# Diagonal tiles on ScalarE in eight instructions a stage, and seven products in the last seven pairs

## The chip, the cores and the metric

The kernel runs on one core of one Trainium2 chip. The metric is the device time of one execution in microseconds, the median over several executions. TensorE, VectorE, ScalarE, GpSimd and SyncE (SP) each work through a queue of their own, in order, and wait for one another by semaphores.

## The reference

A linear attention with decay (per head and channel) is followed by a two-layer network with a leaky ReLU:

```python
# r, k, v: (B=4, H=8, S=768, D=48); w, u: (H, D)
for t in range(S):
    cur = np.einsum('bhd,bhe->bhde', u[None] * kt, vt)
    y[:, :, t] = np.einsum('bhd,bhde->bhe', rt, state + cur)
    state = w[None, :, :, None] * state + np.einsum('bhd,bhe->bhde', kt, vt)
x = y as (B * S = 3072, H * D = 384)
h = x @ w_in                    # 384 x 2048
g = np.maximum(0.01 * h, h)
out = g @ w_out                 # 2048 x 384
```

The inputs and the output are float32; the kernel computes in bfloat16 with float32 accumulation.

## The kernel before

The 3072 rows are 24 stages (n) of 128 tokens, six for each of the four batches. A stage works on all eight heads. Two stages make a pair (m = n // 2, 12 pairs), and the network runs on pairs.

The work of a stage n is:

- `prep(n)` scales r and k by powers of the decay into `qk`; for n >= 8 (`TURNED`) a DMA transpose on SP's queue turns them into `tp`, for earlier stages TensorE and ScalarE do (`turn`).
- `prep2(n)` finds `s`, the weight of a token on its own value (the u term). For n < 8 (`DIAG`) it comes out of a product on TensorE. For n >= 8 VectorE computes it in three instructions (ku at L342, rku at L344, the sum `s_tok` at L346; two buffers of each, by n % 2), and `diag_tile(n)` writes a diagonal matrix with `s` for each head into the tile `at[n % 6]`: two GpSimd instructions (L354), each for four heads, that multiply the identity by `s`.
- `a_mm(n)` makes the scores of the eight heads on TensorE (L391), in two PSUM banks that lie side by side for n >= 8, and `a_mask(n)` moves those below the diagonal into `at` (VectorE, L401). It keeps what the tile has on the diagonal, so it comes after `diag_tile(n)`.
- `y_part(n)` multiplies `at` and the running state into y (L508), and ScalarE evicts it to `xT` (L528).
- `kv_mm(n)` and `state(n)` update the state (L425, L475 to L480); the last stage of a batch has none.

The network of a pair: `g1_pair(m, j)` for j = 0 to 7 is the first product, 48 matmuls in all (L558), each j into a bank of its own, which ScalarE evicts through the leaky ReLU (Prelu) into `gT` (L564). The second product is `second(m)`: for the pairs in `SEVEN` it is `g2_seven(m)`, else `g2(2m)` and `g2(2m + 1)`, 16 matmuls of 384 columns each (L575), evicted to `out_sb` by ScalarE (L581) and stored by SP. `g2_seven` computes the same with seven block products in place of eight, 56 matmuls of 192 columns (L639). It needs four sums of blocks of `gT` for each pair (`g_sum`, VectorE, L613), four sums of blocks of `w_out` made once (`w_sum`, L595), three evictions on ScalarE that are kept aside (`keep`, L647), three additions on VectorE that go to the output (`plus`, L670) and one plain eviction.

All instructions are written down in one order, from which each engine takes its own; waits follow from the keys that an operation reads and writes. `ORDER` writes out the start by hand, up to stage 9's scores and pair 2's first half of the second product. Then a loop runs over the pairs m = 3 to 11. In before, an iteration is: the first product of pair m; `prep2` of stages 2m + 4 and 2m + 5 (`ahead`); `g_sum` of pair m - 1 if that is in `SEVEN`; loads of stages 2m + 8 and 2m + 9 on GpSimd's queue, paced by the first product; `a_mm` and `a_mask` of `ahead`; `y_part` of stages 2m + 2 and 2m + 3; `kv_mm` and `state` of `ahead`; `prep` of stages 2m + 6 and 2m + 7; `w_sum`; and `second(m - 1)`.

The eight PSUM banks go round: every product takes the next bank (`next_bank`), and waits there for whoever still reads what that bank held. `a_mm` leaves bank 7 out where its two banks would not lie side by side (L383). Ahead of `second` the counter is turned on to the bank that y began with:

```python
        if m < NST // 2 - 1:
            while taken[0] % 8 != y_first:
                taken[0] += 1
```

Of the kernel before, what the change touches and what calls it, by code (L numbers as in the profile page):

```python
# [5 lines left out]
ALU = mybir.AluOpType  # L6
AF = mybir.ActivationFunctionType
# [4 lines left out]
B, H, S, D = 4, 8, 768, 48  # L12
# [3 lines left out]
NST = B * NC  # L16
HD = H * D
E = 64
NP = H // 2
# [4 lines left out]
FIRST, EARLY = 6, 2  # L24
# [96 lines left out]
def bass_rwkv5_eagle__then__act_leaky_relu_kernel(  # L121
# [15 lines left out]

    NQK, NTP, NVS, NAT, NT, NX, NG, NO, NRK = 6, 6, 6, 6, 6, 3, 3, 4, 14
    TURNED, DIAG = 8, 8
    SEVEN = (8,9,10,11)  # L140
    HF, NH = NFB // 2, HD // 2
    w_in_sb = SB("w_in_sb", [128, NSL, DFF])
    w_out_sb = SB("w_out_sb", [128, NFB, HD])
# [24 lines left out]
    ident = SB("ident", [128, 128])  # L168
    ku = [SB(f"ku{i}", [128, HD]) for i in range(2)]
    rku = [SB(f"rku{i}", [128, HD]) for i in range(2)]  # L170
    s_tok = [SB(f"s_tok{i}", [128, H], FP32) for i in range(2)]
# [3 lines left out]
    at = [SB(f"at{i}", [128, 2, NP, 128]) for i in range(NAT)]  # L175
# [11 lines left out]
    V, A, PE, SP, G = nc.vector, nc.scalar, nc.tensor, nc.sync, nc.gpsimd  # L187
    sch = Sched(ctx, nc)
    add = sch.add
# [79 lines left out]
    for name in LOADS.split():  # L269
# [12 lines left out]
        R=["tcol"], W=["kexp"])  # L282
    add("dve", lambda: V.tensor_scalar(qexp[:, :], tcol[:, :], 1.0, float(-MID), ALU.mult, ALU.add),
        R=["tcol"], W=["qexp"])
    add("dve", lambda: V.memset(v_sb[:, :, :].rearrange("p n (h e) -> p (n h) e", e=E)[:, :, D:E], 0.0), W=["v0"])
    add("dve", lambda: V.tensor_tensor(wu_row[:, :], w_row[:, :], u_row[:, :], ALU.mult),
        R=["w_row", "u_row"], W=["wu_row"])
    for i in range(NQK):
# [6 lines left out]
        R=["one_row", "w_row"], W=[key_w, "bc"])  # L295
# [33 lines left out]
        add("dve", lambda: V.tensor_tensor(prod[i2][:, :, :], tp[it][:, 0:NP, :], tp[it][:, NP:2 * NP, :], ALU.mult),  # L329
            R=[("tp", it, 0), ("tp", it, 1)], W=[("prod", i2)])  # L330

    def prep2(n):
        i2, iv = n % 2, n % NVS
        if n < DIAG:
            ps_s, key = kv_bank[n]
            s_of = ps_s[:, HD:HD + H]
            add("dve", lambda: V.tensor_tensor(hd(vs[iv][:, :]),
                                               v_sb[:, n, :].rearrange("p (h e) -> p h e", e=E)[:, :, 0:D],
                                               s_of.unsqueeze(2).to_broadcast([128, H, D]), ALU.mult),
                R=[("v", n), key], W=[("vs", iv)])  # L340
        else:
            add("dve", lambda: V.tensor_tensor(ku[i2][:, :], k_of(n), u_tab[:, :], ALU.mult),  # L342
                R=[("k", n % NRK), "u_tab"], W=[("ku", i2)])
            add("dve", lambda: V.tensor_tensor(rku[i2][:, :], r_of(n), ku[i2][:, :], ALU.mult),  # L344
                R=[("r", n % NRK), ("ku", i2)], W=[("rku", i2)])
            add("dve", lambda: V.tensor_reduce(s_tok[i2][:, :], hd(rku[i2][:, :]), AX.X, ALU.add),  # L346
                R=[("rku", i2)], W=[("s", i2)])
            diag_tile(n)

    def diag_tile(n):  # L350
        ia = n % NAT
        for hh in range(2):
            s_of = s_tok[n % 2][:, :].rearrange("p (m two) -> p two m", two=2)[:, hh, :]
            add("pool", lambda hh=hh, s_of=s_of: G.tensor_tensor(  # L354
                at[ia][:, hh, :, :], ident[:, :].unsqueeze(1).to_broadcast([128, NP, 128]),
                s_of.unsqueeze(2).to_broadcast([128, NP, 128]), ALU.mult),
                R=["ident", ("s", n % 2)], W=[("at", ia, hh)])

    def turn(n):
        it, iq = n % NTP, n % NQK  # L360
# [251 lines left out]
        ][i]  # L612
        add("dve", lambda: V.tensor_tensor(x[i][:, :, :], a, b, op), R=keys, W=[("gs", m % 2, i)])  # L613

    def g2_seven(m, early=(), late=()):
        ig, i2 = m % NG, m % 2
        final = m == NST // 2 - 1
        banks = [next_bank() for _ in range(4 if final else 3)]
        top, low = slice(0, HF), slice(HF, NFB)
        one, two = slice(0, NH), slice(NH, HD)  # L620

        def product(where, left, right, first, last):
            ps_o, key = banks[where]
            if isinstance(left, int):
                lhs, reads = gs[i2][left], [("gs", i2, left)]
            else:
                r, c = left
                lhs = gT[ig][:, HF * c:HF * c + HF, 128 * r:128 * r + 128]
                reads = [("gT", ig, r, j) for j in range(4 * c, 4 * c + 4)]
            if isinstance(right, int):  # L630
                rhs = tw[right]
                reads = reads + [("tw", right)]
            else:
                rhs = w_out_sb[:, right[0], right[1]]
                reads = reads + [("wout", i) for i in range(4)]

            def emit():
                for s in range(HF):
                    done = PE.matmul(ps_o[:, 0:NH], lhs[:, s, :], rhs[:, s, :], start=first and s == 0,  # L639
                                     stop=s == HF - 1, skip_group_check=not (first and last))  # L640
                return done

            add("pe", emit, R=reads, W=[key])

        def keep(where, i):
            ps_o, key = banks[where]
            add("act", lambda: A.activation(snap[i2][i][:, :], ps_o[:, 0:NH], AF.Copy), R=[key], W=[("snap", i2, i)])  # L647

        def store(r, c):
            n = 2 * m + r  # L650
            io, cols = n % NO, (one, two)[c]
            if final:
                add("sp", lambda: SP.dma_start(out[128 * n:128 * n + 128, cols], out_sb[io][:, cols]),
                    R=[("o", io, c)], W=[("out", n, c)], dma=f"o{io}{c}")
            elif (n, 1 - c) in landed:
                add("sp", lambda: SP.dma_start(out[128 * n:128 * n + 128, :], out_sb[io][:, :]),
                    R=[("o", io, 0), ("o", io, 1)], W=[("out", n, 0)], dma=f"o{io}")
            landed.append((n, c))

        def plain(where, r, c):  # L660
            ps_o, key = banks[where]
            io, cols = (2 * m + r) % NO, (one, two)[c]
            add("act", lambda: A.activation(out_sb[io][:, cols], ps_o[:, 0:NH], AF.Copy), R=[key],
                W=[("o", io, c)])
            store(r, c)

        def plus(where, i, r, c, after=()):
            ps_o, key = banks[where]
            io, cols = (2 * m + r) % NO, (one, two)[c]
            add("dve", lambda: V.tensor_tensor(out_sb[io][:, cols], ps_o[:, 0:NH], snap[i2][i][:, :], ALU.add),  # L670
                R=[key, ("snap", i2, i), *after], W=[("o", io, c)])
            store(r, c)

        landed = []
        def both(where, i, j):
            ps_o, key = banks[where]
            add("dve", lambda: V.tensor_tensor(snap[i2][i][:, :], ps_o[:, 0:NH], snap[i2][j][:, :], ALU.add),
                R=[key, ("snap", i2, j)], W=[("snap", i2, i)])

        if not final:  # L680
            product(0, (0, 0), (top, one), True, False)
            keep(0, 0)
            product(1, 0, 0, True, False)
            keep(1, 1)
            product(0, 1, 1, False, False)
            keep(0, 2)
            for i in early:
                g_sum(m + 1, i)
            product(2, (0, 1), (low, one), True, True)
            plus(2, 0, 0, 0)  # L690
            product(0, 2, 2, False, False)
            plus(0, 1, 1, 1)
            product(1, 3, (low, two), False, True)
            plus(1, 2, 0, 1)
            for i in late:
                g_sum(m + 1, i)
            product(0, (1, 1), 3, False, True)
            plain(0, 1, 0)
            return
        product(0, (0, 0), (top, one), True, False)  # L700
        keep(0, 0)
        product(1, 2, 2, True, False)
        keep(1, 3)
        product(2, 0, 0, True, False)
        both(2, 1, 3)
        product(0, 1, 1, False, True)
        keep(0, 2)
        plus(0, 1, 1, 1, after=[("snap", i2, 2)])
        product(1, (1, 1), 3, False, True)
        plus(1, 2, 1, 0)  # L710
        product(2, 3, (low, two), False, True)
        plus(2, 2, 0, 1)
        product(3, (0, 1), (low, one), True, True)
        plus(3, 0, 0, 0)
# [8 lines left out]
             "G": g1, "J": g1_pair, "H": g2, "L": lambda n: load_stage(n, pace=[("pace", (n - 4) // 2, (n - 4) % 2)])}  # L723
    for name in ORDER.split():
        steps[name[0]](*(int(x) for x in name[1:].split(".") if x))
    def second(m, early=(), late=()):
        if m in SEVEN:
            g2_seven(m, early, late)
        else:
            g2(2 * m)  # L730
            g2(2 * m + 1)

    for m in range(FIRST // 2, NST // 2):
        for j in range(8):
            g1_pair(m, j)
        ahead = [n for n in (2 * m + 4, 2 * m + 5) if n < NST]
        for n in ahead:
            prep2(n)
        if m - 1 in SEVEN:
            for i in (0, 1, 3, 2):  # L740
                g_sum(m - 1, i)
        for n in (2 * m + 8, 2 * m + 9):
            if n < NST:
                load_stage(n, pace=[("pace", 2 * m, 0)])
# [16 lines left out]
        for n in (2 * m + 6, 2 * m + 7):  # L761
            if n < NST:
                prep(n)
        if 4 <= m < 8:
            w_sum(m - 4)
        if m < NST // 2 - 1:
            while taken[0] % 8 != y_first:
                taken[0] += 1
        if m == NST // 2 - 1:
            second(m - 1, (2, 0), (1, 3))  # L770
        else:
            second(m - 1)
    second(NST // 2 - 1)

    last_out = [o for o in sch.ops if o.dma is not None and o.dma.startswith("o")]
# [56 lines left out]
```

## Time and profile before

| | us |
|---|---|
| median of 3 runs (169.91 to 170.51) | 169.96 |
| the profiled execution's own time | 170.25 |
| its span in the trace | 168.5 |
| TensorE busy in the span | 162.8 |
| VectorE busy | 115.2 |
| GpSimd busy | 103.8 |
| ScalarE busy | 93.4 |

The profile is of one execution. Its page gives the busy time of each engine, the chain of work that ended last (followed back from the last instruction to what released each one), and groups of instructions by line, with shapes, counts, busy time and mean length. L346 is line 346 of the kernel before. PE is TensorE, DVE VectorE, ACT ScalarE, POOL GpSimd, PEld TensorE's loading of weights. The trace behind the page gives the chain and each engine's instructions in order of time: start, length, engine, line, and what they write and read; several of a kind in a row are merged into one line with their number.

### The profile page before, as it was taken

How to read it: one execution, taken by the hardware profiler on the slowest of the kernel's cores; microseconds unless marked ns; L12 is line 12 of the kernel's file. 1: busy time of each engine (PE TensorE's matmuls, PEld its weight loads, DVE VectorE, ACT ScalarE, POOL GpSimd, SP SyncE). 2: the span in 40 equal slices, each digit the busy share in tenths (PEclk: the TensorE clock that was granted, in tenths of full speed). 3: DMA queues.
4: the chain of work that ended last, by engine and by line, in shares of the span. 5: the costliest groups of instructions: out<-in, count | busy, mean ns of one | idle time of the engine just before them, and what ended most of it. 6: DMA issues, size and time to landing. Idle time of an engine off the chain costs nothing.

```text
span 168.5 us, 5112 instructions
## 1 busy us (share of the span) xinstructions
PE 162.8 (97%) x2203; PEld 128.9 (77%) x2203; DVE 115.2 (68%) x211; ACT 93.4 (55%) x176; POOL 103.8 (62%) x117
## 2 busy tenths in 40 slices
PE   6799999999999999999999999999999999999994
PEld 1568898889656876876866867867867898898993
DVE  7699776752998969379379399099199977036253
ACT  4753888789112851952843933924834845828520
POOL 7999999991379799792992995983605600000000
PEclk9999999999999999999999999999999999999999
DMA  5999999999999979999699599699207202002022
GB/s 97 116 156 166 169 155 173 200 184 143 129 226 146 158 44 116 224 77 115 176 66 152 145 67 146 150 104 180 83 0 144 77 4 93 0 4 95 4 93 93
DMA packets 99258, 19.66 MB, mean 117 GB/s; under 512 B 92322, under 2 KB 99236, under 8 KB 99236
## 3 DMA queue, kind: packets, MB, share of 16 engines
q0 software_dynamic: 76512, 10.03, 90.9%
q1 hardware_dynamic: 21682, 9.11, 25.1%
q8 instruction: 17, 0.28, 0.7%
q10 hardware_dynamic: 1042, 0.20, 0.6%
q14 instruction: 5, 0.04, 0.1%
HBM read 20.45 MB, written 4.72 MB: 149 GB/s over the span
## 4 chain that ended last, share of the span: by engine, by line
PE 93%; POOL 4%; ACT 1%; issue 1%; DVE 0%; POOLq 0%
PE ps_all L558 31%; PE ps_all L575 25%; PE ps_all L639 11%; PE ps_all L541 7%; PE ps_all L508 6%; PE ps_all L391 4%; PE ps_all L367 3%; PE ps_all L425 3%; POOL rk_sb L217 2%; PE ps_all L513 1%; ACT tp L378 1%; POOL v_sb L217 1%; PE ps_all L430 1%; PE ps_all L421 1%; POOL w_in_sb L227 0%
## 5 line engine op out<-in xcount | busy, mean ns | idle before, releaser
L558 PE MATMUL ps_all<-xT,w_in_sb 128*128 128x256 bf16 x480 | 54.5, 273 | 0.0
L354 POOL TENSOR_TENSOR at<-ident,s_tok 128x512 bf16<-128x512 bf16 x32 | 35.0, 1122 | 28.6 <-DVE s_tok L346 28.6
L558 PEld LDWEIGHTS ps_all<-xT,w_in_sb 128*128 128x128 bf16 x480 | 46.7, 98 | 6.2
L564 ACT ACTIVATE gT<-ps_all 128x512 bf16<-128x512 f32 x80 | 47.8, 598 | 5.7 <-PE ps_all L558 1.2
L575 PE MATMUL ps_all<-w_out_sb,gT 128*128 128x384 bf16 x256 | 43.3, 326 | 0.0
L575 PEld LDWEIGHTS ps_all<-w_out_sb,gT 128*128 128x128 bf16 x256 | 24.5, 98 | 15.6
L401 DVE CAST_PREDICATED at<-mask,ps_all 128x1024 bf16<-128x1024 uint16 x16 | 18.8, 1220 | 20.3 <-PE ps_all L391 20.3
L581 ACT ACTIVATE out_sb<-ps_all 128x384 f32<-128x384 f32 x16 | 7.9, 492 | 37.9 <-PE ps_all L575 37.9
L217 POOL DMA_DIRECT2D v_sb<-in_v_dram x24 | 22.6, 946 | 0.4 <-issue 0.4
L217 POOL DMA_DIRECT2D rk_sb<-in_k_dram x23 | 21.7, 942 | 0.0
L217 POOL DMA_DIRECT2D rk_sb<-in_r_dram x23 | 21.4, 930 | 0.0
L344 DVE TENSOR_TENSOR rku<-rk_sb,ku 128x384 bf16<-128x384 bf16 x16 | 13.8, 861 | 0.5
L528 ACT ACTIVATE xT<-ps_all 128x384 bf16<-128x384 f32 x24 | 11.0, 491 | 4.9 <-PE ps_all L508 3.0
L541 PE MATMUL ps_all<-xT,w_in_sb 128*128 128x128 bf16 x192 | 13.0, 225 | 0.0
L670 DVE TENSOR_TENSOR out_sb<-ps_all,snap 128x192 f32<-128x192 f32 x13 | 4.6, 357 | 11.8 <-PE ps_all L639 11.1
L541 PEld LDWEIGHTS ps_all<-xT,w_in_sb 128*128 128x128 bf16 x192 | 11.7, 101 | 0.5 <-issue 0.2
L409 DVE TENSOR_TENSOR at<-ps_all,mask 128x512 bf16<-128x512 f32 x16 | 10.3, 683 | 2.4 <-PE ps_all L391 2.4
L546 ACT ACTIVATE gT<-ps_all 128x512 bf16<-128x512 f32 x16 | 9.6, 598 | 3.8 <-PE ps_all L541 3.1
L508 PE MATMUL ps_all<-at,v_sb 128*32 128x128 bf16 x384 | 11.2, 226 | 0.0
L378 ACT ACTIVATE tp<-ps_all 128x512 bf16<-128x512 f32 x15 | 8.2, 595 | 3.7 <-PE ps_all L367 3.7
L508 PEld LDWEIGHTS ps_all<-at,v_sb 128*32 128x32 bf16 x384 | 8.3, 98 | 2.2 <-issue 0.5
L508 PE MATMUL ps_all<-tp,st 128*32 128x128 bf16 x240 | 9.6, 221 | 0.0
(80 smaller groups left out, 196.9 us busy)
## 6 DMA issues: line engine op xcount, KB each, us to landing
out_dram<-out_sb SPq DMA_DIRECT2D x22, 192.0 KB, 2.6
v_sb<-in_v_dram POOLq DMA_DIRECT2D x24, 96.0 KB, 5.3
rk_sb<-in_r_dram POOLq DMA_DIRECT2D x23, 96.0 KB, 5.0
rk_sb<-in_k_dram POOLq DMA_DIRECT2D x23, 96.0 KB, 4.3
w_in_sb<-in_moe_w_in_dram POOLq DMA_DIRECT2D x4, 384.0 KB, 6.5
w_out_sb<-in_moe_w_out_dram POOLq DMA_DIRECT2D x4, 384.0 KB, 10.0
out_dram<-out_sb SPq DMA_DIRECT2D x4, 96.0 KB, 1.6
tp<-qk SPq DMA_TRANSPOSE x16, 4.2
```

Of the source, the lines that this page charges most:

```text
L217: add("pool", lambda: G.dma_start(dst, src), R=pace, W=[key], dma=f"{which}{n}")
L344: add("dve", lambda: V.tensor_tensor(rku[i2][:, :], r_of(n), ku[i2][:, :], ALU.mult), R=[("r", n % NRK), ("ku", i2)], W=[("rku", i2)])
L354: add("pool", lambda hh=hh, s_of=s_of: G.tensor_tensor(at[ia][:, hh, :, :], ident[:, :].unsqueeze(1).to_broadcast([128, NP, 128]), s_of.un ...
L401: add("dve", lambda: V.copy_predicated(at[n % NAT][:, :, :, :].rearrange("p two m i -> p (two m) i"), mask[:, :].bitcast(mybir.dt.uint16). ...
L409: add("dve", lambda hh=hh, part=part: V.tensor_tensor(at[n % NAT][:, hh, :, :], part, mask[:, :].unsqueeze(1).to_broadcast([128, NP, 128]) ...
L508: last = PE.matmul(ps_y[32 * q:32 * q + 32, 128 * s:128 * s + 128], a, m, start=first_mm and (s == 0 or n >= DIAG), stop=last_mm and n >= ...
L528: add("act", lambda: A.activation(xT[m % NX][:, :, 128 * half:128 * half + 128], ps_y[:, 0:HD].rearrange("p (s t) -> p s t", t=128), AF.Copy),
L541: last = PE.matmul(ps_g[:, 128 * f:128 * f + 128], w_in_sb[:, s, 128 * fb:128 * fb + 128], xT[ix][:, s, t], start=s == 0, stop=s == NSL - 1)
L558: last = PE.matmul(ps_g[:, 256 * f:256 * f + 256], w_in_sb[:, s, 128 * fb:128 * fb + 128], xT[ix][:, s, :], start=s == 0, stop=s == NSL - 1)
L564: add("act", lambda: A.activation(gT[ig][:, 2 * j:2 * j + 2, :].rearrange("p f t -> p (f t)"), ps_g[:, :], AF.Prelu, alpha=0.01), R=[key], ...
L575: last = PE.matmul(ps_o[:, 0:HD], gT[ig][:, s, 128 * half:128 * half + 128], w_out_sb[:, s, :], start=s == 0, stop=s == NFB - 1)
L639: done = PE.matmul(ps_o[:, 0:NH], lhs[:, s, :], rhs[:, s, :], start=first and s == 0, stop=s == HF - 1, skip_group_check=not (first and last))
```

## The change

The diagonal tiles of a stage are written by ScalarE, with one instruction for each head: a copy of the 128 x 128 identity scaled by `s_tok`, a value for each partition. For the iterations m = 3 and 4 `prep2` of the two stages ahead, with its tiles, stands inside the first product, behind j = 1 and j = 3. From m = 4 on, `s` is computed one pair further ahead (stages 2m + 6 and 2m + 7, behind `g_sum`), and the sixteen tiles are written in `second(m - 1)`: ahead of a plain second product, or spread over the start of `g2_seven` (two, one, one, and twelve). `SEVEN` grows from pairs 8 to 11 to pairs 5 to 11, and the four `w_sum` go to m = 3, 4 and 5.

```diff
--- before.py
+++ after.py
@@ -137,7 +137,7 @@
 
     NQK, NTP, NVS, NAT, NT, NX, NG, NO, NRK = 6, 6, 6, 6, 6, 3, 3, 4, 14
     TURNED, DIAG = 8, 8
-    SEVEN = (8,9,10,11)
+    SEVEN = (5, 6, 7, 8, 9, 10, 11)
     HF, NH = NFB // 2, HD // 2
     w_in_sb = SB("w_in_sb", [128, NSL, DFF])
     w_out_sb = SB("w_out_sb", [128, NFB, HD])
@@ -329,7 +329,7 @@
         add("dve", lambda: V.tensor_tensor(prod[i2][:, :, :], tp[it][:, 0:NP, :], tp[it][:, NP:2 * NP, :], ALU.mult),
             R=[("tp", it, 0), ("tp", it, 1)], W=[("prod", i2)])
 
-    def prep2(n):
+    def prep2(n, whole=True):
         i2, iv = n % 2, n % NVS
         if n < DIAG:
             ps_s, key = kv_bank[n]
@@ -345,16 +345,15 @@
                 R=[("r", n % NRK), ("ku", i2)], W=[("rku", i2)])
             add("dve", lambda: V.tensor_reduce(s_tok[i2][:, :], hd(rku[i2][:, :]), AX.X, ALU.add),
                 R=[("rku", i2)], W=[("s", i2)])
-            diag_tile(n)
-
-    def diag_tile(n):
+            if whole:
+                diag_tile(n)
+
+    def diag_tile(n, heads=range(H)):
         ia = n % NAT
-        for hh in range(2):
-            s_of = s_tok[n % 2][:, :].rearrange("p (m two) -> p two m", two=2)[:, hh, :]
-            add("pool", lambda hh=hh, s_of=s_of: G.tensor_tensor(
-                at[ia][:, hh, :, :], ident[:, :].unsqueeze(1).to_broadcast([128, NP, 128]),
-                s_of.unsqueeze(2).to_broadcast([128, NP, 128]), ALU.mult),
-                R=["ident", ("s", n % 2)], W=[("at", ia, hh)])
+        for h in heads:
+            add("act", lambda h=h: A.activation(at[ia][:, h % 2, h // 2, :], ident[:, :], AF.Copy,
+                                                scale=s_tok[n % 2][:, h:h + 1]),
+                R=["ident", ("s", n % 2)], W=[("at", ia, h % 2)])
 
     def turn(n):
         it, iq = n % NTP, n % NQK
@@ -612,7 +611,7 @@
         ][i]
         add("dve", lambda: V.tensor_tensor(x[i][:, :, :], a, b, op), R=keys, W=[("gs", m % 2, i)])
 
-    def g2_seven(m, early=(), late=()):
+    def g2_seven(m, early=(), late=(), tiles=()):
         ig, i2 = m % NG, m % 2
         final = m == NST // 2 - 1
         banks = [next_bank() for _ in range(4 if final else 3)]
@@ -677,13 +676,21 @@
             add("dve", lambda: V.tensor_tensor(snap[i2][i][:, :], ps_o[:, 0:NH], snap[i2][j][:, :], ALU.add),
                 R=[key, ("snap", i2, j)], W=[("snap", i2, i)])
 
+        def some(lo, hi):
+            for n, h in tiles[lo:hi]:
+                diag_tile(n, [h])
+
         if not final:
             product(0, (0, 0), (top, one), True, False)
+            some(0, 2)
             keep(0, 0)
+            some(2, 3)
             product(1, 0, 0, True, False)
             keep(1, 1)
+            some(3, 4)
             product(0, 1, 1, False, False)
             keep(0, 2)
+            some(4, 16)
             for i in early:
                 g_sum(m + 1, i)
             product(2, (0, 1), (low, one), True, True)
@@ -723,22 +730,27 @@
              "G": g1, "J": g1_pair, "H": g2, "L": lambda n: load_stage(n, pace=[("pace", (n - 4) // 2, (n - 4) % 2)])}
     for name in ORDER.split():
         steps[name[0]](*(int(x) for x in name[1:].split(".") if x))
-    def second(m, early=(), late=()):
+    def second(m, early=(), late=(), tiles=()):
         if m in SEVEN:
-            g2_seven(m, early, late)
+            g2_seven(m, early, late, tiles)
         else:
+            for n, h in tiles:
+                diag_tile(n, [h])
             g2(2 * m)
             g2(2 * m + 1)
 
     for m in range(FIRST // 2, NST // 2):
+        ahead = [n for n in (2 * m + 4, 2 * m + 5) if n < NST]
+        further = [n for n in (2 * m + 6, 2 * m + 7) if n < NST and m > FIRST // 2]
         for j in range(8):
             g1_pair(m, j)
-        ahead = [n for n in (2 * m + 4, 2 * m + 5) if n < NST]
-        for n in ahead:
-            prep2(n)
+            if m < FIRST // 2 + 2 and j in (1, 3):
+                prep2(ahead[j // 2])
         if m - 1 in SEVEN:
             for i in (0, 1, 3, 2):
                 g_sum(m - 1, i)
+        for n in further:
+            prep2(n, False)
         for n in (2 * m + 8, 2 * m + 9):
             if n < NST:
                 load_stage(n, pace=[("pace", 2 * m, 0)])
@@ -761,15 +773,15 @@
         for n in (2 * m + 6, 2 * m + 7):
             if n < NST:
                 prep(n)
-        if 4 <= m < 8:
-            w_sum(m - 4)
+        for i in {3: (0, 1), 4: (2,), 5: (3,)}.get(m, ()):
+            w_sum(i)
         if m < NST // 2 - 1:
             while taken[0] % 8 != y_first:
                 taken[0] += 1
         if m == NST // 2 - 1:
             second(m - 1, (2, 0), (1, 3))
         else:
-            second(m - 1)
+            second(m - 1, tiles=[(n, h) for n in further for h in range(H)])
     second(NST // 2 - 1)
 
     last_out = [o for o in sch.ops if o.dma is not None and o.dma.startswith("o")]
```

## The prediction, made before the change was run

> **What bounds the kernel now.** I read the page first (busy shares, shares of the chain), then the chain in order of time, then the groups, then ScalarE's and VectorE's timelines. Page, and two groups that the change touches:
>
> ```profile
> PE 162.8 (97%) x2203; PEld 128.9 (77%) x2203; DVE 115.2 (68%) x211; ACT 93.4 (55%) x176; POOL 103.8 (62%) x117
> PE 93%; POOL 4%; ACT 1%; issue 1%; DVE 0%; POOLq 0%
> L354 POOL TENSOR_TENSOR at<-ident,s_tok 128x512 bf16<-128x512 bf16 x32 | 35.0, 1122 | 28.6 <-DVE s_tok L346 28.6
> L575 PE MATMUL ps_all<-w_out_sb,gT 128*128 128x384 bf16 x256 | 43.3, 326 | 0.0
> ```
>
> TensorE is busy 97% of the span and carries 93% of the chain. GpSimd's tiles (35.0 us) are not on the chain: what they cost is hidden. So the change can gain only by shortening TensorE's own work, and loses wherever it makes TensorE wait. The chain in order of time (start, length) gives one iteration of the loop over pairs, m = 3, the start of m = 4, and the last two products:
>
> ```profile
> 54.83 5.24 PE ps_all L558 x48
> 60.07 0.55 PE ps_all L391 x16
> 60.62 0.90 PE ps_all L508 x56
> 61.51 0.28 PE ps_all L425 x4
> 61.79 5.30 PE ps_all L575 x32
> 67.09 5.24 PE ps_all L558 x48
> ...
> 74.23 5.20 PE ps_all L575 x32
> ...
> 135.33 4.93 PE ps_all L639 x56
> ...
> 146.60 4.86 PE ps_all L639 x56
> ...
> 156.70 9.32 PE ps_all L639 x112
> ```
>
> The pieces of an iteration touch: first product 5.24, scores 0.55, y 0.90, state product 0.28, second product 5.30. From the start of g1 to the start of second is 61.79 - 54.83 = 6.96 us at m = 3 and 74.23 - 67.09 = 7.14 us at m = 4 (two state products there). ScalarE's and VectorE's timelines (start, length) give the price of small ScalarE work:
>
> ```profile
> 4.88 0.61 ACT L297 ACTIVATE tab<-lnw,qexp 128x384 bf16<-128x384 f32 x1
> 5.40 0.60 ACT L298 ACTIVATE tab<-lnw,kexp 128x384 bf16<-128x384 f32 x1
> 8.90 1.08 ACT L378 ACTIVATE tp<-ps_all 128x512 bf16<-128x512 f32 x2 [0.35 <-PE ps_all L367]
> 55.52 5.18 ACT L564 ACTIVATE gT<-ps_all 128x512 bf16<-128x512 f32 x8 [0.16 <-PE ps_all L558]
> 61.17 0.88 ACT L528 ACTIVATE xT<-ps_all 128x384 bf16<-128x384 f32 x2 [0.47 <-PE ps_all L508]
> 54.66 0.36 DVE L344 TENSOR_TENSOR rku<-rk_sb,ku 128x384 bf16<-128x384 bf16 x1
> 55.91 2.23 DVE L344 TENSOR_TENSOR rku<-rk_sb,ku 128x384 bf16<-128x384 bf16 x1
> ```
>
> Back to back, ScalarE starts the next instruction before the last one ends: two evictions of 512 columns take 1.08 us, so the second starts 0.49 us after the first though each lasts 0.595 us.
>
> **What a tile costs on ScalarE.** No ACTIVATE of 128 columns is in the trace. The slope is (598 - 331) / (512 - 192) = 0.834 ns a column (evictions at L564 and L647). The nearest rows in form are L297 and L298: SBUF to SBUF with a scale by partition. They start 0.52 us apart at 384 columns; 256 columns fewer take 0.213 us off: 0.307 us from tile to tile (lasting 0.39 each). The ends: 0.18 us (the two 48x4 evictions of L457 start that far apart), and 0.39 if nothing overlapped. I take 0.307, from the rows with the same operands. A stage of eight is then 2.46 us on ScalarE, against 2.24 on GpSimd, and a pair is 4.91 us.
>
> The Trainium skill, page "ScalarE: Activation LUTs", section "What ACT_TABLE_LOAD costs", gives 280 ns + 0.833 ns a column with a pointer operand and 93 ns of overlap, which makes an estimate of 0.294 us; the stalls below would then be 5.9 us in place of 6.2.
>
> **Edit 1: tiles inside the first product, m = 3 and 4.** The diff puts prep2 of the two stages ahead behind g1_pair 1 and 3, so ScalarE's order becomes two Prelu, eight tiles, two Prelu, eight tiles, four Prelu, two xT. TensorE does not wait for Prelu while it has banks, but the next products reuse them. Counting next_bank from the start: at m = 3, g1 takes banks 5, 6, 7, 0, 1, 2, 3, 4; the scores of stage 10 take 5, 6, those of 11 take 0, 1 (7 is skipped) and so wait for Prelu j = 4; y(8), y(9) take 2, 3, and second's first product takes 2 again, so it waits for xT(8), which stands behind all sixteen tiles.
>
> At m = 3, Prelu j = 1 starts at 55.52 + 0.655 = 56.17. Then 0.49 to the first tile, 16 x 0.307 = 4.91 of tiles, 2 x 0.49 for j = 2, 3, 4 x 0.49 for j = 4 to 7, 0.49 for xT(8): 65.00. Before, second starts at 61.79: **3.2 us lost**. The s of both stages is no obstacle: s_tok(10) is done at 55.61, and s_tok(11) by about 56.9, as rku takes 0.36 and not 2.23 without a tile running on GpSimd beside it.
>
> At m = 4 the same sum from g1's start is 1.34 + 0.49 + 4.91 + 0.98 + 1.96 + 0.49 = 10.17 us against 7.14: **3.0 us lost**. Here y(10) and y(11) wait for Prelu j = 4, 5, and second for xT(10). VectorE has s_tok(12) in time: scores(11) end near 63.4, then mask 1.2, state 0.9, two qk 1.0, two w_sum 1.9, prep2 1.25, so about 70; wanted at g1's start (70.3) + 1.83 = 72.1.
>
> In terms of the pitch p the two stalls are 16p - 1.7 and 16p - 1.88.
>
> **Edit 2: tiles one pair ahead in second, m = 4 to 8.** At m = 4 sixteen more tiles (4.91) and two evictions (0.8) run beside a plain second of 5.20, after xT(11) 0.3 us into it: ScalarE is free 0.8 us into the next g1, whose first Prelu is ready after 0.66. Prelu bunch at 0.49 against 0.655 from TensorE, so the lag is gone in one or two of them: nothing. With seven products (m = 6 to 8), tiles 4.91 and four evictions of 192 columns at about 0.24 make 5.9 beside some 4.75, so g1 begins with ScalarE about 1 us behind; first Prelu 0.5 us late, made up at 0.165 each by j = 4; the scores want j = 1 to 4 only at 5.24. Nothing again. The first keep stands behind two tiles (0.61) and is ready after 0.66: nothing. ScalarE's least for such a pair is 3.9 + 0.8 + 4.9 + 1.0 = 10.6 against TensorE's 11.7; the cover is 1.1 us a pair, gone at p = 0.37. The tiles of 8 and 9, in the written order, fall where ScalarE waits 2.3 to 2.8 us before each out_sb eviction (L581): nothing.
>
> **Edit 3: VectorE's side.** New: 3 pairs x (four g_sum of 0.69 to 0.87, three sums of 0.36). Gone: the slow rku (mean 861 against 360, 16 times, 8 us). Before the mask in pairs 7 and 8 stand g_sum 2.8 and prep2 2.5, 5.3 us from g1's start; the scores come at 5.5. Nothing, with 0.2 us to spare; if that is gone, the product in the state's bank waits, as it did once for sum_t (0.19 us). Prep2 waits at m = 4 for the tiles that still read s_tok (two buffers), with masks 12 and 13 behind it until about 78.5; y(12) wants them at 91.
>
> **Edit 4: GpSimd.** It keeps only its loads, which start at their pace and no longer behind 28.6 us of waits for s; earlier loads help nobody, since no compute waits for them after the start.
>
> **Edit 5: seven products in pairs 5, 6, 7.** Plain second takes 5.30, 5.20, 5.20 here; seven products take 9.32 / 2 = 4.66 undisturbed and 4.86 to 4.93 with short waits. 5.30 - 4.8 + 2 x (5.20 - 4.75) = **1.4 us gained**, bounds 1.0 to 1.7. On the SP queue the stores of these pairs wait for the end of second; the next transposes come behind them only after the next g1, so none is held up. The w_sum are moved to m = 3 to 5, ahead of their first use at m = 6.
>
> **Sum.** 168.5 + 3.2 + 3.0 - 1.4 = 173.3 of span; 1.75 lies around it (170.25 - 168.5): 175.05. The profiled run stands 0.29 above the median 169.96, so I predict 174.8.
>
> **Rivals.**
> *The stall is not there (faster).* The tiles pay only if p is so short that ScalarE still reaches xT in time: 32p - 3.6 < 1.4, p below 0.156 us. Then the time is down to 169.96 - 1.4 = 168.6. Against: even 4 columns take 0.16 us (L457), and the tiles have 128 and a scale pointer. 0.05.
> *A tile starts every 0.18 to 0.2 us.* Stalls 2.2 to 2.8, total +0.8 to +1.4: 171. It would need the scale pointer and the SBUF read to be free. 0.05.
> *No overlap, p = 0.39.* Stalls 8.9, and pairs 6 to 8 lose about 0.2 us each: 169.96 + 8.9 - 1.4 + 0.6 = 178.1. Against it, L297 and L298 do overlap. 0.10.
> *The matmul clock falls in the stalls.* The trace has TensorE at half rate early: 12 matmuls of L541 take 1.28 us at 14.5 and 0.67 from 17.6 on; from 7.3 to 16.4 this costs some 4.5 us. If one stall brought this back: 174.8 + 4.5 = 179.3. For it: 2.8 us unbroken at m = 3 and 2.5 at m = 4 with little work after. Against it: no mid-kernel gap in this trace shows it. 0.08. By the Trainium skill, page "TensorE: Matmul & The Clock Gate", section "Why this matters for your kernels", idle gaps of more than about 3 us between bursts of matmuls should be avoided, since one idle window brings half rate back; no run shown here has such a gap in mid-kernel.
>
> **How the numbers follow.** Forecast 0.72, rivals 0.05, 0.05, 0.10, 0.08. The low end is p = 0.25 with the gain at 1.7 (about 172.6), the high end no overlap (178.1). One measurement here tells about 0.5% from no change. Within 0.5% (0.85 us) of no change needs p between 0.13 and 0.18: that is 0.01 of the first rival and 0.03 of the second. The other 0.04 of the first is faster by more; all else, 0.92, is slower.
>
> **What would show it.** ScalarE: 128 tiles near 390 ns, 0.3 apart. The chain: some 6 us of ScalarE (gT, xT, at) at 60 to 65 and 76 to 81, TensorE idle there; L639 with 392 matmuls, L575 with 160; rku at 0.36; GpSimd 35 us less busy. Wrong if TensorE runs through both places, or if it waits for ScalarE in pairs 6 to 8 too.

## The result: slower by 4.7%

The changed kernel takes 178.19 us (median of 4 runs, 176.46 to 179.06) against 169.94 for the kernel before (4 runs): a ratio of 1.047, 95% interval 1.039 to 1.056. The prediction said slower, 174.8 us, with a range up to 178.1; the measured median lies 0.1 us above that end. The profiled execution is the fastest of the four: 176.46 us, 174.7 us of span. It had one fall of the matmul clock to half rate (mean granted clock 0.990); the other three show 0.981, as much as two such falls make.

From the page of the kernel after:

```profile
PE 162.9 (93%) x2275; PEld 133.4 (76%) x2275; DVE 114.9 (66%) x232; ACT 128.2 (73%) x310; POOL 68.8 (39%) x85
PE 74%; ACT 9%; DMA 7%; DVE 6%; POOL 2%; issue 2%; POOLq 0%; DVEq 0%
L354 ACT ACTIVATE at<-ident,s_tok 128x128 bf16<-128x128 bf16 x128 | 39.4, 393 | 2.6 <-DVE s_tok L346 2.6
```

TensorE's share of the chain is down from 93% to 74%, and ScalarE, DMA and VectorE now stand in it. TensorE is busy for as long as before (162.9 us and 162.8), in a span 6.2 us longer. Here is the chain in order of time at m = 3, at m = 4 and at the end of pair 7 (the lines named here, but for L315 and L354, have numbers one lower than before):

```profile
55.10 1.32 PE ps_all L557 x12
...
57.05 2.33 ACT at L354 x8
59.38 0.96 ACT gT L563 x2
60.34 2.34 ACT at L354 x8
62.67 0.97 ACT gT L563 x2
...
65.03 5.38 PE ps_all L574 x32
70.40 1.32 PE ps_all L557 x12
...
79.76 0.75 PE ps_all L424 x8
80.51 6.30 PE ps_all L574 x32
...
117.86 4.69 PE ps_all L638 x56
...
132.28 0.64 DVE qk L315 x2
...
133.21 0.63 DVE out_sb L669 x2
...
133.88 0.83 PE ps_all L638 x8
134.72 5.24 PE ps_all L557 x48
```

At m = 3 the way from g1 to second goes through two Prelu, eight tiles, two Prelu, eight tiles, as the prediction wrote it down: 65.03 - 55.10 = 9.93 us where it was 6.96, so 2.97 lost. At m = 4 it is 80.51 - 70.40 = 10.11 against 7.14, also 2.97, and then the second product takes 6.30 and not 5.20. TensorE's timeline shows what the scores of stages 9 and 11 and y(10) wait for:

```profile
52.00 0.40 PE L390 MATMUL ps_all<-tp 48*128 48x128 bf16 x8 [0.72 <-DMA tp<-qk]
63.21 0.40 PE L390 MATMUL ps_all<-tp 48*128 48x128 bf16 x8 [2.54 <-ACT gT L563]
78.50 0.24 PE L507 MATMUL ps_all<-at,v_sb 128*32 128x128 bf16 x4 [2.31 <-ACT gT L563]
```

The windows of the two pairs (length, busy time of PE, PEld, DVE, ACT, POOL, then the granted clock, and two figures on the DMA) show that the clock fell in the second one, 0.90 on the mean:

```profile
55.10:70.40 15.30, 12.68 (x159) 9.21 (x157) 8.68 (x16) 10.48 (x28) 5.26 (x6) 1.00 1.28 127
70.40:86.81 16.41, 14.10 (x163) 10.08 (x161) 11.02 (x22) 15.03 (x44) 5.25 (x6) 0.90 0.95 96
```

A mean of 0.990 over 174.7 us is 3.4 us at half rate.

### The profile page after: what moved, and what is told of

It reads as the page before. It is cut to its first block, busy times and chain, and to the rows that moved or that the text cites. A ratio compares the mean times of both kernels' runs of the same rounds, so it can differ in the third digit from the quotient of the medians.

```text
span 174.7 us, 5382 instructions
## 1 busy us (share of the span) xinstructions
PE 162.9 (93%) x2275; PEld 133.4 (76%) x2275; DVE 114.9 (66%) x232; ACT 128.2 (73%) x310; POOL 68.8 (39%) x85
## 4 chain that ended last, share of the span: by engine, by line
PE 74%; ACT 9%; DMA 7%; DVE 6%; POOL 2%; issue 2%; POOLq 0%; DVEq 0%
PE ps_all L557 26%; PE ps_all L638 17%; PE ps_all L574 11%; PE ps_all L540 6%; ACT at L354 5%; PE ps_all L507 5%; DMA tp<-qk 4%; PE ps_all L390 3%; ACT gT L563 3%; DMA rk_sb<-in_k_dram 3%; PE ps_all L424 2%; POOL rk_sb L217 1%; PE ps_all L366 1%; DVE at L400 1%; PE ps_all L512 1%
## 5 line engine op out<-in xcount | busy, mean ns | idle before, releaser
L557 PEld LDWEIGHTS ps_all<-xT,w_in_sb 128*128 128x128 bf16 x480 | 46.7, 98 | 5.8
L354 ACT ACTIVATE at<-ident,s_tok 128x128 bf16<-128x128 bf16 x128 | 39.4, 393 | 2.6 <-DVE s_tok L346 2.6
L574 PE MATMUL ps_all<-w_out_sb,gT 128*128 128x384 bf16 x160 | 28.3, 335 | 0.0
L574 PEld LDWEIGHTS ps_all<-w_out_sb,gT 128*128 128x128 bf16 x160 | 15.6, 100 | 10.5 <-issue 1.2
L638 PE MATMUL ps_all<-tw,gs 128*128 128x192 bf16 x168 | 16.0, 246 | 0.0
L638 PEld LDWEIGHTS ps_all<-tw,gs 128*128 128x128 bf16 x168 | 14.0, 98 | 0.0
L346 DVE TENSOR_REDUCE s_tok<-rku 128x8 f32<-128x384 bf16 x16 | 8.8, 553 | 5.9 <-ACT at L354 4.8
L390 PE MATMUL ps_all<-tp 48*128 48x128 bf16 x192 | 9.1, 229 | 3.5 <-ACT gT L563 2.5
L580 ACT ACTIVATE out_sb<-ps_all 128x384 f32<-128x384 f32 x10 | 4.7, 484 | 9.7 <-PE ps_all L574 9.7
L638 PE MATMUL ps_all<-w_out_sb,gT 128*128 128x192 bf16 x112 | 11.6, 246 | 0.2 <-ACT xT L527 0.2
```

The costliest lines, as they stand in the source:

```text
L354: add("act", lambda h=h: A.activation(at[ia][:, h % 2, h // 2, :], ident[:, :], AF.Copy, scale=s_tok[n % 2][:, h:h + 1]), R=["ident", ("s" ...
L390: last = PE.matmul(at_bank[n][hh][0][:, 128 * p:128 * p + 128], tp[it][rows, NP + p, :], tp[it][rows, p, :], start=True, stop=True)
L557: last = PE.matmul(ps_g[:, 256 * f:256 * f + 256], w_in_sb[:, s, 128 * fb:128 * fb + 128], xT[ix][:, s, :], start=s == 0, stop=s == NSL - 1)
L574: last = PE.matmul(ps_o[:, 0:HD], gT[ig][:, s, 128 * half:128 * half + 128], w_out_sb[:, s, :], start=s == 0, stop=s == NFB - 1)
```

## The experiments

**The tiles of stages 10 to 13 back on GpSimd.** The stall is undone, all else stays.

```diff
     def diag_tile(n, heads=range(H)):
         ia = n % NAT
+        if n in (10, 11, 12, 13):
+            for hh in range(2):
+                ...   # the two GpSimd instructions of the kernel before
+            return
         for h in heads:
```

> The tiles of stages 10 to 13, which the change puts between the Prelu of the first product at m = 3 and 4, go back to GpSimd (two instructions a stage); the tiles of 8, 9 and 14 to 23 stay on ScalarE, seven products stay in pairs 5 to 11. Theory (the sixteen tiles ahead of the last Prelu hold up TensorE at m = 3 and 4, and the matmul clock falls in that hold-up): both stalls (2.97 us each in the profile after) and the 1.35 us at half clock in pair 4 go, 174.7 - 7.3 = 167.4 us of span, about 169.2 us, clock 1.0. Rival (ScalarE's tiles cost wherever they stand, also beside the second product): only a part comes back, 172 us or more.

Measured: 170.18 us (10 runs), 1.001 times the kernel before (0.998 to 1.004), clock 1.0 in every run. 8.0 us came back, so the 96 tiles that stay on ScalarE, nearly all of them beside a second product, cost next to nothing there, and the rival falls: the iterations m = 4 and 5, with sixteen tiles beside a plain second product, take 12.34 and 12.16 us here and 12.34 and 12.17 before. The result is 1 us more than expected. The wait of the scores of stage 9 for their transpose (0.73 us) and the late additions of pair 7 are still there, but they were in the 174.7 too. The traces give two other reasons: the pairs m = 3 and 4 give back 7.11 us and not 7.3 (15.30 and 16.41 become 12.26 and 12.34), and the change's profiled run, from which the expectation started, reached m = 3 early, at 55.10 us where this run did at 55.99.

**Half of those tiles on GpSimd.** The same edit with `n in (11, 13)`.

> The change with the tiles of stages 11 and 13 on GpSimd: eight tiles in place of sixteen stand between the Prelu of the first product at m = 3 and 4. Theory (the stall is the number of tiles times the pitch, less 1.7 and 1.9 us that TensorE has to spare there; pitch 0.291 in the profile after): 8 x 0.291 - 1.7 = 0.6 us at m = 3 and 0.4 us at m = 4, no gap long enough for the clock to fall: 1.0 us more than with all four stages on GpSimd (170.2), so 171.2 us, clock 1.0. Rival (any tile there costs its full length): half of the 2.97 us stalls, 3 us in all: 173.

Measured: 171.08 us (10 runs), 0.9 more than with all four on GpSimd; mean clock 0.999 to 1.0. Its chain:

```profile
55.45 1.32 PE ps_all L565 x12
...
57.40 2.33 ACT at L362 x8
59.73 1.94 ACT gT L571 x4
...
63.07 5.37 PE ps_all L582 x32
68.44 1.32 PE ps_all L565 x12
...
76.06 5.37 PE ps_all L582 x32
```

From g1 to second 7.62 us at both places: 0.66 and 0.48 lost, where the rule "tiles times pitch less what TensorE can spare" gave 0.6 and 0.4. Half the tiles cost a fifth, not half: the first 1.7 us are free.

**A fixed scale for the tiles of 10 to 13.**

```diff
-                                                scale=s_tok[n % 2][:, h:h + 1]),
+                                                scale=0.5 if 10 <= n < 14 else s_tok[n % 2][:, h:h + 1]),
```

> The change, but the tiles of stages 10 to 13 take a fixed scale of 0.5 and not s by partition, so the u term of these four stages is another; number and place of the instructions are the same. Theory (the pitch is what decides): by the Trainium skill's page on ScalarE, section on ACT_TABLE_LOAD's cost, a scale by partition adds 93 ns, so the pitch goes from 0.291 to 0.20; the stalls are then 16 x 0.2 - 1.7 = 1.5 and 1.3 us, the clock stays at 1.0, and the time is 170.2 + 2.8 = 173 us. Rival (the number of instructions decides, not their form): pitch 0.29, 178 us with the clock falling.

Measured: 172.78 us (4 runs), clock 1.0. Its chain shows eight tiles in 1.59 us, a pitch of 0.199. One of these tiles lasts 300 ns (median), one with a scale by partition 391 in the same run:

```profile
55.96 1.32 PE ps_all L557 x12
...
57.91 1.59 ACT at L354 x8
...
64.43 5.37 PE ps_all L574 x32
```

8.47 us from g1 to second at m = 3, so 1.51 lost, as 16 x 0.2 - 1.7 says; at m = 4 the same 8.47 (69.80 to 78.27) make 1.33. With the same number of instructions, the pitch decides. For a pointer operand the Trainium skill, page "ScalarE: Activation LUTs", section "What ACT_TABLE_LOAD costs", gives 93 ns; the trace agrees, with 91 ns between 391 and 300.

**TensorE kept busy through the wait.**

```diff
-            for p in range(NP):
+            for p in [p for _ in range({10: 9, 13: 9}.get(n, 1)) for p in range(NP)]:
```

> The change, with the scores of stages 10 and 13 computed nine times each (the same values into the same banks), 2.2 us of matmuls that fill TensorE's wait at m = 3 and at m = 4. Theory (the clock falls because TensorE idles there): granted clock 1.0 in all runs, no half rate, 174.7 to 175.3 us, 3 us less than the change's usual run. Rival (the falls have another cause, or cost nothing): clock stays at 0.98 to 0.99 and the time at 178 us; if the filling is not hidden, more.

Measured: 176.13 us (4 runs, 175.85 to 177.07), clock 1.0 in all, 2.06 us under the change. TensorE's timeline at m = 3:

```profile
60.77 2.18 PE L390 MATMUL ps_all<-tp 48*128 48x128 bf16 x72
63.70 0.40 PE L390 MATMUL ps_all<-tp 48*128 48x128 bf16 x8 [0.75 <-ACT gT L563]
```

The wait is filled and the clock does not fall, in any run; both pairs now take 15.30 us. So the idle TensorE is the cause of the falls, and two of them cost about 2.06 us. The expected 174.7 to 175.3 was too low by 1: it took a whole 1.7 us off the change's profiled run for its one fall, and a fall is worth less (pair 4 took 16.41 us there, so 1.1); and that run had reached m = 3 0.5 us earlier than this one (55.10 and 55.59).

**Seven products alone**, on the kernel before.

```diff
-    SEVEN = (8,9,10,11)
+    SEVEN = (5, 6, 7, 8, 9, 10, 11)
...
-        if 4 <= m < 8:
-            w_sum(m - 4)
+        for i in {3: (0, 1), 4: (2,), 5: (3,)}.get(m, ()):
+            w_sum(i)
```

> The kernel before with seven products in pairs 5 to 11 and the earlier w_sum, tiles on GpSimd and s as before. Theory (TensorE alone counts): 1.2 to 1.5 us less than before, 168.6 us. Rival (VectorE is too late with GpSimd's tiles beside it: four g_sum and a prep2 of 3.3 to 4.5 us ahead of the masks, which the scores want at 5.5): masks 0.6 to 1.7 us late, so the state and the additions come late and second waits 0.3 to 1 us in pairs 5 to 7: 169.5 to 171 us.

Measured: 173.34 us (4 runs), 1.019 times before (1.014 to 1.024): the rival is right, and by more than it said. VectorE's timeline, in pair 6's iteration:

```profile
108.84 1.42 DVE L613 TENSOR_TENSOR gs<-gT,gs 128x1024 bf16<-128x1024 bf16 x1
110.18 0.68 DVE L613 TENSOR_TENSOR gs<-gT 128x1024 bf16<-128x1024 bf16 x1
110.78 2.34 DVE L401 CAST_PREDICATED at<-mask,ps_all 128x1024 bf16<-128x1024 uint16 x2
```

Beside GpSimd's tiles a g_sum takes 1.42 us; in the change, with no tile beside it, the same sum takes 0.69. The masks begin 1.35 us after the scores are done (109.43), and the products wait for the state and the additions. In this order of instructions the seven products pay only where GpSimd writes no tiles beside their sums: the two halves of the change belong together. The Trainium skill, page "SBUF — State Buffer", section "SBUF: two separate sides", says that a VectorE instruction with two SBUF inputs and a GpSimd one that reads SBUF exclude each other; the trace agrees, and here it costs 0.73 us in two of the four sums of the pair.

**Tiles alone:** the change with `SEVEN = (8, 9, 10, 11)`.

> The change with seven products in pairs 8 to 11 only, as before; the tiles as in the change. Theory: the gain of the seven products (0.5 us each in pairs 5 and 6, none in pair 7, 0.14 in pair 8) is not there: 1.0 to 1.2 us more than the change, 179 us with two falls of the clock, 177.5 with one. Rival (the seven products themselves cost, since ScalarE is fuller): the same as the change or less, 176 to 178.

Measured: 178.81 us (4 runs, 177.38 to 179.37), 0.6 over the change; of the runs with one fall of the clock its span is 175.6 against 174.7, and of those with two it is 176.9 to 177.6 against 176.4 to 177.2. The direction is the theory's; the falls blur the size, and by itself this run settles little.

**The loads of stages 12 and 13 held back**, on top of the first experiment.

```diff
-                R=[("rku", i2)], W=[("s", i2)])
+                R=[("rku", i2)], W=[("s", i2), ("sdone", n)])
...
-             ... "L": lambda n: load_stage(n, pace=[("pace", (n - 4) // 2, (n - 4) % 2)])}
+             ... "L": lambda n: load_stage(n, pace=[("pace", (n - 4) // 2, (n - 4) % 2)] + ([("sdone", 9)] if n > 11 else []))}
```

> As the run with the tiles of stages 10 to 13 on GpSimd, but the loads of stages 12 and 13 wait until s of stage 9 is there. Since the tiles of 8 and 9 left GpSimd these loads start at 38 us where they started at 50.5 before, and the transposes of stages 8 and 9 are issued at 42.6 to 45 us; the scores of stage 9 waited 0.7 us for theirs. Theory (the loads and the transposes share the transfer engines and collide): the transpose of stage 9 lands in under 6.4 us in place of 7.2, no wait at the scores of 9, 0.7 us less: 169.5 us. Rival (the transpose takes that long anyway): 170.2.

Measured: 169.63 us (10 runs), 0.55 less than without, 0.996 times before (0.994 to 0.999). DMA issues from 42 to 54 us (count, size, median us to landing), first of the kernel after, then of this one:

```profile
rk_sb<-in_r_dram POOLq DMA_DIRECT2D x1, 96.0 KB, 15.5
tp<-qk SPq DMA_TRANSPOSE x4, 7.3
```

```profile
rk_sb<-in_r_dram POOLq DMA_DIRECT2D x2, 96.0 KB, 5.4
tp<-qk SPq DMA_TRANSPOSE x3, 3.4
```

These two views don't hold the same transposes, since in the second one the fourth comes after 54 us. The two that count, of stages 8 and 9, are those issued between 42 and 48 us: they land in 7.0 us (median) in the change, in 6.9 with the tiles of stages 10 to 13 on GpSimd, in 3.2 here (3.0 and 3.4) and in 4.4 in the kernel before. The scores of stage 9 no longer wait, so the rival falls. The next two transposes, which now run beside the loads that were held back, take 7.2 and 7.0 us; the scores of pair 5 at m = 3 take 0.68 us for 0.55, whether because of that is not shown.

**The two qk of pair 8's prep ahead of g_sum**, on top of that: at m = 8 `prep(22)` and `prep(23)` stand ahead of the g_sum in place of behind the states.

> A version meant to be better than both: the tiles of 10 to 13 on GpSimd, the late loads of 12 and 13, and at m = 8 the two qk of prep ahead of g_sum in place of behind the states. Theory: the additions of pair 7 waited in VectorE's order behind masks, states and the two qk (1.0 us), which held up TensorE's last product by 0.55 us; with the qk ahead VectorE begins the masks 0.3 us later but reaches the additions 0.65 us earlier, and pair 7 gains what pairs 5 and 6 gain: 0.5 us less than with the late loads alone: 169.0 us, 0.6% under the kernel before. Rival (the masks become late in turn and the product in the state's bank waits): the same as the late loads alone.

Measured: 168.98 us (11 runs, 168.00 to 169.76), 0.992 times the kernel before (0.990 to 0.995): 0.8% under it, and better than the change. Pair 7's second product takes as long as pair 6's (L646 is L638 of the change):

```profile
110.88 4.69 PE ps_all L646 x56
...
122.54 4.68 PE ps_all L646 x56
```

## Why the prediction was right, and where it was off

The table sets the medians in a row, from the last version back to the change. Each step is the difference of two medians, so that they add up is no test; the traces are the test of the single steps.

| step | us | from |
|---|---|---|
| kernel before, beside the experiments | 170.21 | 28 runs |
| last version: seven products in pairs 5 to 7, most tiles on ScalarE | -1.23 | 168.98 |
| additions of pair 7 late behind two qk | +0.65 | 169.63 |
| loads of 12 and 13 beside the transposes of 8 and 9 | +0.55 | 170.18 |
| sixteen tiles in g1, m = 3 and 4 | +5.95 | 176.13 |
| two falls of the matmul clock | +2.06 | 178.19 |

The last line compares with the change's own runs, made beside a kernel before of 169.94; that sets the accuracy of the sum at some 0.3 us. In the traces the tiles in g1 cost 6.0 us (15.30 and 15.30 for 12.26 and 12.34), the wait for the transpose 0.72, pair 7's late additions 0.52, and the one fall of the profiled run 1.1.

The direction and its cause, the stall, came out as forecast. That the time lies near the high end of the range is luck: that end stands for tiles that don't overlap on ScalarE (a pitch of 0.39), and the pitch measured is 0.291. The time got there by the clock, which was no part of the sum, and by the loads.

- *The stall, its place and its form*: right. 3.2 and 3.0 were predicted, 2.97 and 2.97 measured; of the second, 0.18 us is the half-rate clock, since with the clock at 1.0 (the filled wait) the same way takes 80.82 - 70.89 = 9.93 us and not 10.11. The pitch was 0.291 us (2.33 for eight), where 0.307 was taken from L297 and L298. The sentence from the Trainium skill, page "ScalarE: Activation LUTs", had a pitch of 0.294, which is nearer; both stalls by it are 5.8 us by the prediction's own formulas (it wrote 5.9), and 5.76 were measured without the half-rate clock.
- *The clock*: the step that failed. It was a rival at 0.08 for one fall of 4.5 us. It came in every run of the change, once or twice, and costs 1.0 us each: 3.4 us at half rate, of which a part lies in the stall itself. The price from the start of the kernel (9.1 us of half rate) was too high and the chance too low. The reason given against it, that no gap in the middle of the trace before shows a fall, had no weight: TensorE's longest wait there, once the start is over, is 0.2 us, so that trace couldn't show one. Without the falls the time is 176.1, 1.3 above the forecast; 0.7 of that is the wait for the transpose, and the rest is not taken apart.
- *Seven products*: 1.4 us predicted, 1.23 in the last version, where the scores take 0.13 and 0.17 us more at m = 3 and 5; in the change the pairs' iterations are shorter by 0.51 (12.26 to 11.75), 0.52 (12.34 to 11.82), 0.00 (12.17 both) and 0.14 for pair 8, where sum_t no longer comes late.
- *VectorE's 0.2 us to spare*: the masks came in time, as said (VectorE waits 0.66 us for the scores at m = 8). What was left out is the end of its order: two states, two qk and only then the additions that the last product waits for. Pair 7 gained nothing for it, where pairs 5 and 6 gained 0.5.
- *GpSimd, "earlier loads help nobody"*: wrong in its sign. The loads of 12 and 13 started at 38.2 us in place of 50.5 and ran beside the transposes, which the scores of stage 9 wait for: 0.55 us, a term that the sum put at nothing.
- *ScalarE free again by the next g1, beside the second product*: right. In pairs 5 to 7 no product waits for it.

## What to carry to other kernels

An engine that is free on average still must not be given work ahead of an eviction that frees a PSUM bank which another engine is about to need: count the banks, find the first product that reuses one, and see what stands before its eviction in the evicting engine's order. The same work was free behind that point. A resource that is freed is a change as well: ask what starts earlier for it, and with what that collides.

## What the runs showed of the hardware

- In the change TensorE waits 2.54 us at m = 3 and 2.31 at m = 4, each time with some 1.5 us of small products after it, and the matmul clock falls to half: once in the profiled run, and by the mean clock of 0.981 twice in the three others. Waits of 1.05 and 0.83 us (with the fixed scale) did not, and 2.2 us of matmuls in the wait prevented it. The Trainium skill, page "TensorE: Matmul & The Clock Gate", section "Why this matters for your kernels", warns of gaps of more than about 3 us: here a shorter one, followed by a little work, was enough.
- The length of a wait does not decide alone. In the profiled run of the change the longer wait, at m = 3, brought no fall, and the shorter one, at m = 4, did. The fall lasts 3.41 us, from 79.21 to 82.62. Stretches of that length, counted back from its start, have this busy time of TensorE (then its count of matmuls, the granted clock, and the two figures on the DMA):

```profile
58.73:62.14 3.41, 1.94 (x23) 1.00 2.31 158
62.14:65.55 3.41, 2.25 (x72) 1.00 1.20 67
75.80:79.21 3.41, 1.10 (x59) 1.00 1.96 104
79.21:82.62 3.41, 3.41 (x44) 0.50 0.01 0
```

The wait at m = 3 lies across two of them, which are busy for 1.94 and 2.25 us; the wait at m = 4 lies in one, which is busy for 1.10, and the fall follows. The profiled run with seven products in pairs 8 to 11 only has two falls, again 3.41 us each and 17.07 us apart, five times 3.41; the stretches ahead of them are busy for 0.86 and 1.09 us. So the clock seems to be set in steps of 3.41 us by the work of the step before, and where a step begins would make the difference between one fall and two. That is inferred from three falls; no run here moves the steps against the waits.
- A fall of 3.4 us costs some 1.0 us and not 1.7, half its length. In the profiled run it begins in y(10) and the state products, ahead of a second product that waits for xT(10) anyway (79.78 to 80.27), so only 0.18 us are lost there; the second product then takes 6.30 us, and 5.38 in the run with the filled wait.
- With loads queued ahead, a load of 96 KB landed 15.5 us after its issue and the transposes of stages 8 and 9 took 7.0, against 5.4 and 3.2 with the loads held back.
- A VectorE sum of two bfloat16 tiles (128x1024) takes 1.42 us beside GpSimd's tiles and 0.69 alone.
